# Linear attention and a cosine FFN on one core: another order table for the same steps

## The chip, the cores and the metric

The kernel runs on one core of one Trainium2 chip. The metric is the device time of one execution in microseconds (us); of several executions the median is taken. Engines: PE (TensorE, matmuls), PEld (its weight loads), DVE (VectorE), ACT (ScalarE), POOL (GpSimd) and SP (SyncE, which here issues nearly all DMAs).

## What is computed

Batch 8, 8 heads, 576 tokens a head, head width 64, feature width 128; then a feed-forward part of width 512 to 2048 to 512 over 4608 tokens.

```python
def phi(x):
    proj = np.einsum('bhsd,df->bhsf', x, w_phi)
    proj = proj - np.max(np.abs(proj), axis=-1, keepdims=True)
    return np.concatenate([np.exp(proj), np.exp(-proj)], axis=-1)
q_p, k_p = (phi(q), phi(k))
kv = np.einsum('bhsf,bhsd->bhfd', k_p, v)
z = np.sum(k_p, axis=2)
num = np.einsum('bhsf,bhfd->bhsd', q_p, kv)
den = np.einsum('bhsf,bhf->bhs', q_p, z)[..., None] + 1e-06
x = (num / den)                    # heads side by side: 4608 x 512
h = x @ w_in
g = h * np.cos(h)
out = g @ w_out
```

## The kernel before

The program is first written down as a list of 4103 steps, and nothing is issued while it is written. A step has an engine, a function that issues its instructions, the steps that it needs, and the buffers that it takes or uses: `Step("PE", 0.86, q_mm, [ld], ...)`. Steps are numbered as they are made.

- **Attention**, `attention(u)` for 32 units u of two heads each: steps 0 to 1264, 42 to 39 a unit; the units' qk loads are 0, 42, 83, 124, 165, 206 and so on to 1187 and 1226. A unit loads q and k (`load`, lines 535 to 542, tile `qk`) and v (`load_v`, tile `vs`), projects q (`q_mm`, `q_end`, lines 556 to 562) and k (`k_mm`, `k_end`, lines 597 to 631), takes maxima on DVE, spreads them on POOL, subtracts on POOL (L598), takes exponentials on ACT (`exp_k`, L660 and L663; `exp_q`, L669), and multiplies: `kv_mm` (L709, L715; 32 or 72 narrow matmuls) builds kv and z, `x_mm` (L744, L750; two halves of 32 and 40 narrow matmuls) the output, which DVE divides, transposes and SP stores to `xs` in DRAM.
- **Weights**, `convert(kind, i)`: steps 1265 to 1552. They turn the 64-bit weights into high and low parts of fp32r and store them in DRAM.
- **FFN over three columns of 512 tokens**, `visit(v)`: steps 1553 to 2275. `mm1` (L871, 12 matmuls of 512 columns), then on ACT and DVE `copy`, `reduce`, `cosine`, `times`, `high` and `low`, then `mm2` (L916, L917, 4 matmuls of 512 columns; `one` has 2) and `mm2l` (L923, 2). Partial sums are kept in DRAM (`sums`); `fetch` (L954) loads them, `out_copy` (L959) adds a bank to them and so empties the bank, `out_store` stores them.
- **FFN over six columns in pairs**, `visit_two`: steps 2276 to 4102. With sums of blocks of the operands seven products do the work of eight: `wide` (L1110, 6 matmuls of 512 columns), `turns`, `reduce`, `cosine` and `times`, then `sweep` with `fold_load` (L1267, weights to `wo_h` and `wo_l`), `high`, `low`, `mm2` (L1313, 4) and `mm2l` (L1319, 2).

What sets the order of the work is the list ORDER (lines 88 to 246): a permutation of the 4103 numbers, written out. Steps are issued in that order, so each engine runs its own steps in the order in which ORDER names them, and waits by semaphore for what other engines have to give it. SP's list is a queue in the same way: a DMA whose buffer isn't free holds up those behind it. Buffers turn in rings of one to four (`qk` and `qk_x` one each, `vs` 2, `wo_h` 2, `wo_l` 2, `x_raw` 4, `o` 2), so a load can start when the last reader of the older content is done. `plan()` (line 249) also gives out the eight PSUM banks, along ORDER:

```python
for x in (steps[i] for i in ORDER):
    for b in x.take:
        if b.ring == "bank":
            fit = [i for i in range(len(banks)) if not b.onto or owner[i] and owner[i].kind != "a"]
            b.slot = min(fit, key=lambda i: last(owner[i]))
```

A step gets the bank whose last user stands earliest in ORDER, and waits for that user. ACT holds one table at a time, exp or sin; the loop that issues the steps loads the other one where ORDER asks for it (L1462):

```python
for x in plan():
    if x.eng == "ACT" and x.table not in (None, held_set):
        held_set = x.table
        ACT.preload_act_table(AF.Exp if held_set == "e" else AF.Sin)
    x.fn()
```

PE runs its narrow matmuls on parts of its array; a step of another shape than the one before is a switch of shape.

Steps that the prediction follows: 165, 485 and 1187 are qk loads, and 182, 488 and 1204 are `k_end`, `q_end` and `k_end` of the same units; 289 loads v for the `kv_mm` 317; 2019 is a `fetch` for the `out_copy` 2020 (DVE), 712 an `x_mm` half; 2301 loads a tile of x, 2259 is a `low` (DVE) and 2262 its `mm2l`; 2187 is a `times` (DVE) and 774 a `k_mm`; 3880 and 3881 are `fold_load`s, 3905 the `mm2` that reads 3880. 206, 992 and 2796 are a qk load, another one and a `fold_load`.

Of the kernel before, what the change touches and what calls it, by code (L numbers as in the profile page):

```python
# [26 lines left out]
def phi_attention_then_cos_ffn(ctx: ExitStack, tc: tile.TileContext, qkT, vS, w_phi, w_in, w_out, out, outT):  # L27
# [42 lines left out]
    class Step:  # L70
        def __init__(self, eng, cost, fn, deps=(), take=(), use=(), lat=None, table=None, port=False, kind="", pipe=0.0):
# [10 lines left out]
            for b in self.take + self.use:  # L82
# [6 lines left out]
    ORDER = [0, 3, 5, 4, 7, 8, 6, 9, 10, 11, 42, 58, 60, 62, 44, 1, 12, 46, 2, 17, 19, 18, 23, 24, 1265, 16, 47, 61, 66, 63, 21, 45, 59, 48, 20, 1266, 14, 50, 25,  # L89
# [159 lines left out]
    def plan():  # L249
        place = {steps[x]: i for i, x in enumerate(ORDER)}  # L250
        owner = [None] * len(banks)
# [4 lines left out]

        for x in (steps[i] for i in ORDER):
            for b in x.take:
# [5 lines left out]
                elif b.ring == "v":  # L264
                    b.slot, n_v = n_v, 1 - n_v
        return [steps[i] for i in ORDER]

# [1261 lines left out]
```

## Time and profile before

| | us |
|---|---|
| median of 3 executions (1001.46 to 1005.89) | 1001.76 |
| the profiled execution | 1000.83 |
| its span, first to last instruction | 999.1 |

The profile is of one execution. A page gives busy times by engine, the chain of work that ended last, groups of instructions by line with their mean length and the idle time before them, and DMA issues with the time to landing; the trace behind it gives the timeline of each engine, merged where instructions of one line follow each other, and busy times by stretch. Starts of PE's instructions are recorded, their ends are modelled. TensorE's granted clock was 1.00 throughout.

### The profile page before, as it was taken

The numbers are of one execution on the slowest core, as the hardware profiler recorded it, in microseconds if no ns is written. First come the engines' busy times: TensorE is split into PE (matmuls) and PEld (weight loads), VectorE is DVE, ScalarE is ACT, GpSimd is POOL, SyncE is SP. The second block draws the span as 40 slices with busy tenths as digits, with TensorE's granted clock in tenths as the row PEclk, the third lists the DMA queues.
The fourth block names the chain that finished last, engine by engine and source line by source line (L and its number), as shares of the span: only waits on it lengthen the run. The fifth ranks groups of instructions, "written<-read, shape, count | busy, mean of one in ns | idle before, by whom it ended". The sixth has DMA issues, their size and how long they took to land.

```text
span 999.1 us, 22265 instructions
## 1 busy us (share of the span) xinstructions
PE 985.1 (99%) x8586; PEld 795.6 (80%) x8586; DVE 855.3 (86%) x1494; ACT 769.0 (77%) x1544; POOL 203.3 (20%) x295
## 2 busy tenths in 40 slices
PE   9999999999999999999999999999999999999998
PEld 6778878878888887877788877778878888888786
DVE  7999999999899798777997689987987799776787
ACT  7799999867778866869998779787677775766653
POOL 4564441224332133201223111110200100000000
PEclk9999999999999999999999999999999999999999
DMA  6576788736868675646776546757657485763565
GB/s 234 163 227 179 220 272 287 272 135 226 263 216 274 213 257 188 205 140 247 242 248 198 189 145 197 255 162 256 191 187 231 144 270 182 245 240 102 194 191 187
DMA packets 118745, 211.66 MB, mean 212 GB/s; under 512 B 18672, under 2 KB 61808, under 8 KB 118640
## 3 DMA queue, kind: packets, MB, share of 16 engines
q1 hardware_dynamic: 118496, 210.18, 64.1%
q8 instruction: 67, 1.10, 0.5%
q14 instruction: 38, 0.31, 0.1%
q10 hardware_dynamic: 144, 0.07, 0.0%
HBM read 149.39 MB, written 60.82 MB: 210 GB/s over the span
## 4 chain that ended last, share of the span: by engine, by line
PE 58%; DVE 19%; ACT 11%; DMA 7%; issue 3%; SPq 1%; POOL 1%; DVEq 0%; ACTq 0%; POOLq 0%
PE bank L1110 21%; PE bank L1313 12%; PE bank L1319 6%; PE bank L871 5%; PE bank L744 3%; DVE gl L55 3%; PE bank L709 3%; ACT ek L663 3%; PE bank L605 2%; PE bank L559 2%; DVE bq L594 2%; ACT eq L669 2%; DMA o<-sums 1%; DMA sums<-o 1%; DVE g L895 1%
## 5 line engine op out<-in xcount | busy, mean ns | idle before, releaser
L663 ACT ACTIVATE ek<-bank,mk 128x128 f32<-128x128 f32 x464 | 127.9, 413 | 10.3 <-DVE mk L646 9.9
L598 POOL TENSOR_TENSOR pq<-pq,bq 128x288 f32<-128x288 f32 x128 | 118.5, 954 | 77.9 <-DVE bq L594 59.5
L590 POOL COPY m<-m 32x36 f32<-32x36 f32 x96 | 34.5, 359 | 361.5 <-DVE m L585 357.7
L1313 PE MATMUL bank<-gh,wo_l 128*128 128x512 f32 x336 | 89.3, 394 | 0.4 <-ACT gh L50 0.4
L1313 PE MATMUL bank<-gh,wo_h 128*128 128x512 f32 x336 | 87.4, 394 | 1.3 <-DMA wo_h<-wo_sums 1.3
L669 ACT ACTIVATE eq<-pq 128x576 f32<-128x576 f32 x128 | 80.4, 704 | 3.1 <-POOL pq L598 2.3
L1222 ACT ACTIVATE g<-g,halfpi 128x512 f32<-128x512 f32 x96 | 67.4, 718 | 19.6 <-DVE g L1219 19.3
L1110 PE MATMUL bank<-xh_t,wi 128*128 128x512 f32 x192 | 76.6, 399 | 0.9 <-DVE o L1385 0.3
L744 PEld LDWEIGHTS bank<-kv,eq 128*64 128x64 f32 x2048 | 64.1, 138 | 14.5 <-issue 6.9
L1313 PEld LDWEIGHTS bank<-gh,wo_h 128*128 128x128 f32 x336 | 62.1, 188 | 16.0 <-ACT gh L50 1.9
L1313 PEld LDWEIGHTS bank<-gh,wo_l 128*128 128x128 f32 x336 | 61.9, 188 | 15.4 <-ACT gh L50 2.1
L744 PE MATMUL bank<-kv,eq 128*64 128x65 f32 x2048 | 70.0, 223 | 1.1 <-DVE o L959 1.1
L709 PEld LDWEIGHTS bank<-vs,ek 128*64 128x64 f32 x2048 | 62.7, 138 | 8.3 <-ACT ek L663 1.9
L709 PE MATMUL bank<-vs,ek 128*64 128x65 f32 x2048 | 66.8, 223 | 0.9 <-ACT pq L570 0.9
L1219 DVE SCALAR_TENSOR_TENSOR g<-g,hs 128x512 f32<-128x512 int32 x72 | 51.6, 722 | 13.8 <-ACT g L1216 13.3
L1462 ACT ACT_TABLE_LOAD x48 | 61.6, 1283 | 0.8
L1120 ACT ACTIVATE hs<-bank 128x512 f32<-128x512 f32 x72 | 42.2, 597 | 23.2 <-PE bank L1110 19.1
L1216 ACT ACTIVATE g<-hs 128x512 int32<-128x512 f32 x72 | 45.7, 637 | 17.7 <-DVE hs L1134 11.3
L916 PE MATMUL bank<-wo_h,gh 128*128 128x512 f32 x144 | 57.4, 399 | 0.0
L1110 PE MATMUL bank<-xh_b,wi 128*128 128x512 f32 x144 | 56.9, 395 | 0.0
L1110 PE MATMUL bank<-x_wi,wi 128*128 128x512 f32 x144 | 56.2, 390 | 0.0
L917 PE MATMUL bank<-wo_l,gh 128*128 128x512 f32 x144 | 56.2, 390 | 0.0
(186 smaller groups left out, 2626.0 us busy)
## 6 DMA issues: line engine op xcount, KB each, us to landing
wi<-wi_parts SPq DMA_DIRECT2D x18, 1792.0 KB, 8.1
qk<-qkT SPq DMA_DIRECT2D x31, 640.0 KB, 4.9
wo_h<-wo_sums SPq DMA_DIRECT2D x24, 512.0 KB, 4.5
wo_l<-wo_sums SPq DMA_DIRECT2D x24, 512.0 KB, 4.3
x_raw<-xs SPq DMA_DIRECT2D x47, 256.0 KB, 4.1
wi_parts<-wi SPq DMA_DIRECT2D x12, 896.0 KB, 6.1
vs<-vS SPq DMA_DIRECT2D x32, 325.0 KB, 5.5
wo_l<-wo_parts SPq DMA_DIRECT2D x18, 512.0 KB, 6.0
```

What stands on the lines that cost most here:

```text
L598: qeng.tensor_tensor(out=d["pq"][:, c], in0=d["pq"][:, c], in1=d["bq"][:, c], op=ALU.subtract)
L663: ACT.activation(out=e[:, g, s * P:(s + 1) * P], in_=pk[:, g, :], func=AF.Exp, scale=1.0 - 2.0 * s, bias=d["lk" if s == 0 else "mk", i][:, ...
L669: ACT.activation(out=e[:, s, :], in_=d["pq"][:, j * S:(j + 1) * S], func=AF.Exp, scale=1.0 - 2.0 * s)
L709: PE.matmul(out=acc[c:c + 64, n, i, :], lhsT=e[:, s, P * n + c:P * n + c + 64], rhs=vs[b["v"].slot][:, 2 * s + i, :], start=(s == 0 and i ...
L744: PE.matmul(out=ps[64 * h:64 * h + 64, 65 * g:65 * g + 65], lhsT=d["eq", j][:, n, c:c + 64], rhs=d["kv"][:, 2 * n + j, :], start=h not in ...
L916: PE.matmul(out=bank(acc[tb]), lhsT=n["gh"][:, t], rhs=w[:, 0, r], start=first, stop=False, skip_group_check=True)
L917: PE.matmul(out=bank(acc[tb]), lhsT=n["gh"][:, t], rhs=w[:, 1, r], start=False, stop=False, skip_group_check=True)
L1110: PE.matmul(out=bank(bank_b), lhsT=w[:, part, block, j * P:(j + 1) * P], rhs=d[x, name, j], start=start and k == 0, stop=k == 5, skip_grou ...
L1222: ACT.activation(out=n["g"], in_=n["g"], func=AF.Sin, bias=halfpi, scale=1.0)
L1313: PE.matmul(out=bank(out[j]), lhsT=w[:, place, part, j * P:(j + 1) * P], rhs=n["gh"], start=start and i == mine[0] and part == 0, stop=Fal ...
L1319: PE.matmul(out=bank(out[j]), lhsT=w[:, place, 0, j * P:(j + 1) * P], rhs=n["gl"], start=False, stop=i == mine[-1], skip_group_check=True)
L1462: ACT.preload_act_table(AF.Exp if held_set == "e" else AF.Sin)
```

## The change

One thing changes: the list ORDER. It holds the same 4103 numbers in another sequence, the outcome of a new search over four sets of step lengths in which the lengths of steps of all engines scatter. The steps, their functions, the ring sizes and `plan()` stay. 259 of PE's 1017 steps keep their place in PE's own list; the others move by a few places, 25 at most. On ACT the largest move is 42 places, on DVE 58, on POOL 7 and on SP 64. Since banks and table loads follow from ORDER, some steps get another bank, and the table is loaded at other places. The diff, cut to lines of the list that the prediction speaks of (all other lines of the list change too):

```diff
--- before.py
+++ after.py
@@ -86,164 +86,164 @@
 
     SWITCH = dict(e=1.3, s=1.3, full=0.23, left=0.147, quarter=0.138, upper=0.195)
     SHAPE = dict(mm1="full", mm2="full", mm2l="full", one="full", onel="full", wide="full", k_mm="upper", k_end="full", q_end="full", k_sub="full", kv_mm="left", x_mm="left", q_mm="upper")
-    ORDER = [0, 3, 5, 4, 7, 8, 6, 9, 10, 11, 42, 58, 60, 62, 44, 1, 12, 46, 2, 17, 19, 18, 23, 24, 1265, 16, 47, 61, 66, 63, 21, 45, 59, 48, 20, 1266, 14, 50, 25,
...
-             54, 87, 89, 88, 91, 55, 1272, 34, 35, 90, 104, 69, 72, 57, 73, 165, 182, 108, 101, 74, 106, 109, 1273, 56, 92, 36, 1274, 37, 93, 70, 102, 187, 107,
...
-             314, 203, 368, 261, 289, 293, 296, 262, 308, 240, 332, 239, 260, 312, 241, 259, 309, 277, 242, 278, 345, 275, 274, 331, 279, 297, 1555, 313, 204,
-             1304, 1563, 333, 349, 1305, 347, 348, 281, 317, 1558, 350, 318, 205, 1561, 335, 334, 243, 353, 1564, 354, 298, 299, 302, 280, 330, 303, 316, 1562,
...
-             452, 1629, 422, 453, 436, 462, 1614, 420, 402, 1627, 1628, 1630, 466, 1334, 463, 468, 467, 485, 1612, 1631, 464, 403, 1299, 287, 469, 419, 454, 421,
-             465, 435, 434, 455, 456, 488, 437, 1338, 1339, 1340, 1341, 1336, 447, 471, 1281, 1632, 1644, 472, 470, 1645, 457, 487, 1633, 489, 439, 490, 1646, 404,
...
-             1511, 2145, 672, 2027, 709, 2019, 735, 674, 1512, 2070, 2071, 675, 707, 2020, 676, 1460, 739, 740, 760, 737, 710, 762, 2028, 712, 2029, 677, 711, 713,
...
-             2185, 2186, 2187, 1533, 774, 2134, 2137, 778, 779, 749, 799, 801, 802, 751, 759, 2217, 2152, 776, 750, 752, 753, 754, 1551, 2277, 2135, 2153, 2139,
...
-             2294, 2229, 2230, 2194, 2257, 2303, 2258, 839, 2301, 842, 2240, 2241, 2306, 2312, 2251, 2313, 2307, 2320, 2321, 2267, 2323, 2195, 2308, 2309, 2250,
-             2260, 2310, 2259, 2314, 2311, 2322, 2315, 2317, 2318, 2196, 2252, 2262, 2316, 2264, 843, 841, 844, 845, 2319, 2324, 2327, 2325, 2329, 2328, 2268,
...
-             1152, 2845, 1154, 1138, 2850, 2848, 2852, 1153, 2911, 2839, 1156, 2906, 1139, 1187, 1155, 2909, 1157, 2916, 2854, 2858, 1204, 2851, 1168, 2859, 1158,
...
-             3884, 3878, 3885, 3886, 3888, 3889, 3890, 3891, 3879, 3791, 3898, 3907, 3899, 3792, 3793, 3881, 3893, 3894, 3895, 3900, 3896, 3901, 3902, 3903, 3904,
-             3880, 3905, 3912, 3906, 3877, 3908, 3910, 3913, 3915, 3510, 3928, 3909, 3697, 3914, 3876, 3911, 3917, 4003, 3916, 3932, 3924, 3918, 3920, 3919, 3921,
...
-             4080, 4085, 4050, 4051, 4090, 4092, 4093, 4094, 4095, 4096, 4097, 4098, 4099, 4100, 4101, 4102]
+    ORDER = [0, 3, 5, 4, 7, 8, 42, 58, 6, 9, 10, 44, 1, 62, 45, 60, 17, 46, 1265, 11, 12, 18, 21, 59, 15, 13, 43, 47, 48, 61, 22, 66, 19, 20, 71, 1266, 64, 2, 23,
...
+             86, 72, 1282, 73, 105, 87, 55, 165, 89, 88, 1272, 90, 106, 74, 57, 35, 91, 34, 84, 1273, 70, 54, 92, 1274, 109, 127, 36, 102, 93, 1275, 1276, 141, 69,
...
+             96, 98, 144, 133, 111, 1279, 182, 185, 206, 134, 40, 135, 110, 77, 223, 184, 186, 1283, 187, 78, 189, 188, 125, 79, 228, 145, 168, 80, 167, 191, 1284,
...
+             1302, 259, 289, 308, 260, 307, 1558, 297, 275, 1563, 1303, 277, 1297, 240, 278, 309, 312, 239, 274, 1555, 203, 330, 1304, 345, 241, 349, 347, 279,
+             331, 281, 1305, 1564, 313, 333, 242, 350, 348, 317, 318, 1561, 1306, 319, 280, 123, 334, 1562, 298, 354, 299, 302, 353, 1307, 332, 303, 243, 346, 205,
...
+             1609, 1610, 417, 418, 463, 449, 1329, 1330, 433, 1613, 468, 1621, 448, 1622, 469, 1611, 1331, 365, 450, 1625, 462, 1623, 1332, 452, 464, 485, 451,
+             420, 1624, 453, 1612, 465, 1334, 400, 1629, 1626, 1630, 1627, 1628, 472, 466, 399, 401, 454, 436, 402, 422, 467, 419, 434, 1615, 366, 421, 1631, 488,
...
+             729, 561, 674, 675, 707, 709, 2024, 735, 1510, 1517, 2019, 2026, 760, 2048, 710, 1511, 2073, 712, 2062, 1512, 676, 677, 711, 2049, 737, 730, 738,
+             1514, 762, 2208, 739, 740, 763, 2020, 2078, 1518, 1519, 713, 2079, 714, 743, 2089, 2100, 744, 1424, 761, 764, 2206, 1520, 2050, 715, 2051, 2052, 2053,
...
+             2187, 2276, 2215, 2135, 2188, 749, 2211, 774, 2216, 2217, 2138, 778, 779, 750, 801, 1543, 1544, 1545, 1546, 2176, 2277, 776, 777, 773, 2189, 2139,
...
+             2297, 827, 2200, 841, 2303, 2255, 2256, 2312, 2196, 2313, 2320, 2301, 2307, 2201, 2257, 1551, 2258, 2322, 2251, 2252, 2267, 839, 2202, 2308, 1497,
+             2309, 2310, 2311, 2321, 2317, 842, 2441, 2326, 2259, 2323, 2314, 2315, 2316, 2324, 2327, 2341, 2342, 2264, 2325, 2260, 2329, 2318, 2319, 2343, 2328,
+             2330, 852, 2345, 2337, 2331, 837, 2344, 2338, 2339, 2332, 854, 875, 2262, 2349, 2346, 2333, 2268, 2334, 2350, 855, 2351, 2347, 2352, 2261, 843, 856,
...
+             1170, 2910, 2838, 2906, 2911, 2909, 2839, 1171, 2854, 2847, 2848, 2852, 2849, 2912, 1168, 2856, 1140, 1187, 1174, 1107, 1172, 2907, 1141, 2855, 1069,
+             1169, 2851, 2913, 2858, 1159, 2860, 1173, 2919, 1204, 2853, 2920, 2859, 2917, 1142, 1162, 1143, 1209, 1210, 1190, 1144, 1163, 2857, 1161, 2861, 2864,
...
+             3888, 3912, 3885, 3897, 3973, 3875, 3890, 3889, 3898, 3880, 3893, 3895, 3900, 3894, 3902, 3881, 3903, 3886, 3907, 3908, 3899, 3891, 3896, 3901, 3792,
+             3993, 3913, 3793, 3917, 3876, 3904, 3757, 3877, 3905, 3910, 3511, 3915, 3918, 3988, 3906, 3909, 3920, 3940, 3914, 3911, 3916, 3919, 3928, 3929, 3924,
...
+             4092, 4094, 4090, 4093, 4095, 4097, 4096, 4098, 4099, 4100, 4101, 4102]
     LATENCY = dict(PE=0.35, ACT=0.25, DVE=0.2, POOL=0.25, SP=2.0)
 
     def plan():
```

## Rows read from the trace of the kernel before

**Rows 1.** The page: the span and the busy time of each engine.
```profile
span 999.1 us, 22265 instructions
...
PE 985.1 (99%) x8586; PEld 795.6 (80%) x8586; DVE 855.3 (86%) x1494; ACT 769.0 (77%) x1544; POOL 203.3 (20%) x295
```

**Rows 2.** The chain that ended last (start us, us, what): a stretch of products.
```profile
664.02 14.98 PE bank L1110 x66
```

**Rows 3.** Timeline of PE at ten places: start us, us, instruction, [idle before <-releaser].
```profile
24.98 0.46 PE L630 MATMUL bank<-wphi,qk 128*128 128x128 f32 x2 [0.30 <-DMA qk<-qkT]
...
74.55 2.09 PE L709 MATMUL bank<-vs,ek 128*64 128x65 f32 x64 [0.92 <-ACT pq L570]
...
126.59 0.46 PE L562 MATMUL bank<-qk,wphi 128*128 128x128 f32 x2 [0.39 <-DVE m L584]
...
163.20 0.96 PE L871 MATMUL bank<-xh_b,wi 128*128 128x512 f32 x3
...
339.77 1.15 PE L744 MATMUL bank<-kv,eq 128*64 128x65 f32 x32 [1.06 <-DVE o L959]
...
391.65 1.04 PE L605 MATMUL bank<-wphi,qk 64*128 64x128 f32 x13 [0.67 <-DVE g L902]
...
441.36 0.61 PE L923 MATMUL bank<-wo_h,gl 128*128 128x512 f32 x2
442.99 0.73 PE L923 MATMUL bank<-wo_h,gl 128*128 128x512 f32 x2 [1.02 <-DVE gl L55]
...
652.99 0.46 PE L630 MATMUL bank<-wphi,qk 128*128 128x128 f32 x2 [1.08 <-DMA qk<-qkT]
...
836.89 0.50 PE L1110 MATMUL bank<-xh_t,wi 128*128 128x512 f32 x1 [0.32 <-DVE o L1385]
...
942.67 1.07 PE L1319 MATMUL bank<-gl,wo_l 128*128 128x512 f32 x4
945.03 1.15 PE L1313 MATMUL bank<-gh,wo_h 128*128 128x512 f32 x4 [1.29 <-DMA wo_h<-wo_sums]
```

**Rows 4.** The chain that ended last: five loads in it.
```profile
19.91 4.93 DMA qk<-qkT
...
335.39 3.52 DMA o<-sums
...
436.32 3.91 DMA x_raw<-xs
...
647.03 5.82 DMA qk<-qkT
...
938.78 6.12 DMA wo_h<-wo_sums
```

**Rows 5.** Timeline of PE: two halves of x_mm, then a product.
```profile
513.27 1.15 PE L744 MATMUL bank<-kv,eq 128*64 128x65 f32 x32
...
514.48 1.10 PE L744 MATMUL bank<-kv,eq 128*64 128x65 f32 x32
515.52 1.67 PE L1313 MATMUL bank<-gh,wo_l 128*128 128x512 f32 x6
```

**Rows 6.** The page's DMA issues: count, KB each, median us to landing.
```profile
qk<-qkT SPq DMA_DIRECT2D x31, 640.0 KB, 4.9
wo_h<-wo_sums SPq DMA_DIRECT2D x24, 512.0 KB, 4.5
```

**Rows 7.** The page's groups: table loads (busy us, mean ns, idle before).
```profile
L1462 ACT ACT_TABLE_LOAD x48 | 61.6, 1283 | 0.8
```

**Rows 8.** Timeline of ACT: one table load and what follows.
```profile
413.71 1.28 ACT L1462 ACT_TABLE_LOAD   x1
415.00 1.26 ACT L669 ACTIVATE eq<-pq 128x576 f32<-128x576 f32 x2
```

**Rows 9.** Busy us of each engine by stretch (length, then each engine, clock, DMA).
```profile
0.00:185.00 185.00, 182.04 (x2611) 143.76 (x2612) 169.71 (x330) 168.52 (x377) 80.79 (x126) 1.00 0.69 222
185.00:475.00 290.00, 286.69 (x2271) 233.71 (x2271) 252.30 (x404) 219.81 (x413) 73.36 (x99) 1.00 0.66 222
```

284 rows, old and new, of the table ORDER are left out of this document.

## The prediction

> **What bounds the kernel now.** I read the page's busy times first: PE is busy for 985.1 of 999.1 us, DVE for 855.3, ACT for 769.0 [rows 1]. That looks like a kernel with 14 us to win at most, but the end of a matmul is modelled, so a wait can hide inside "busy". The second view therefore goes by starts: in the chain of waits 66 matmuls of 512 columns take 14.98 us [rows 2], 0.227 us each. Wherever two starts of PE lie further apart than the steps between them need, PE stood still. Laid against this spacing, and against the usual length of each narrow step, PE is late by more than 0.16 us at 20 places, 12.7 us together. One is the first load of the program (0.33 us), which no order removes; 12.4 us are left. The rest of the span is the same matmuls in any order, plus hiccups of about 0.13 us at some hundred places that no step of the table explains. So the change can win 12.4 us at the most, and it can lose as much as it likes.
>
> **Where the 12.4 us lie.** Eight places hold 8.1 us [rows 3]. At 942.67 us four matmuls need 0.91, so the next was due at 943.58; it started at 945.03, 1.45 late. At 441.36 two need 0.45, the next came at 442.99 instead of 441.81, 1.18 late. By the same account 24.98 is 0.37 late, 74.55 is 1.14, 126.59 is 0.66, 339.77 is 1.13, 391.65 is 0.94 and 652.99 is 1.24. Eleven smaller ones of 0.17 to 0.55, from 163.20 to 836.89, make 4.3. What ended the big ones stands in the chain of waits [rows 4]: five times a load landed just before (4.93 us after its issue at 19.91, 3.52 at 335.39, 3.91 at 436.32, 5.82 at 647.03, 6.12 at 938.78); at 339.77 and 442.99 DVE, which the view of rows 3 names, only passed the late load on. The starts 74.55 and 126.59 are named after ACT and DVE, but come 0.14 us after a qk or vs load landed, as 24.98, 652.99 and 945.03 do. Only 391.65 waits for DVE alone.
>
> **The change part by part.** No instruction is added or removed but six table loads; all else is a new order on each engine. I read from the two tables what PE work stands between a load and its first PE reader, and call that its lead.
>
> *Six of the eight places.* Step 1187 (qk load) and its reader 1204 had no PE step between them; now an x_mm half (1.0 us [rows 5]) and an mm2 step (four matmuls, 0.91) stand there: 1.9 us against 1.24 late. 165 and 182 stood side by side; now 15 PE steps are between, six of them of some 1.0 us, against 0.37 late. 3880 and 3905: from nothing to two mm2 and four mm2l, 3.6 us, against 1.45; 3880 also goes ahead of 3881 now instead of behind it. 485 and 488: from one mm1 (2.7) to one mm1, two x_mm halves and a kv_mm, at least 6.0, against 0.66. 2259 and 2262: from one mm2l to over 6 us, against 1.18. Step 712 waited because it took the bank that 2020 empties; 2020 now comes after 712, so plan() gives 712 another bank: 1.13. Sum 6.0 us, if nothing else becomes late.
>
> *Two places stay.* 289 keeps its lead to 317 (7.0 to 6.7 us), and 2187 still stands ahead of 774 with no PE step between: 2.1 us remain. The eleven small waits for DVE and ACT (4.3 us) I leave as they are: the table doesn't thin the chains behind them in one direction.
>
> *What comes instead.* A load with a lead of up to 0.5 us is thin. Without the first three units, the old table has 17 of them and the new 21. Three of the 17 waited for longer than 0.16 us, 3.06 us together, 0.18 per thin load; at that rate the 21 cost 3.8. The other end is zero, and it has a reason: a load that runs ahead of its place in the table is safe if its buffer was freed early. For 165 and 1187 the matmuls between the freeing step and the reader are only 4.8 us against landings of 4.93 and 5.82 [rows 4]. Of the new 21 the shortest, 2796, has 5.2 us, where such a load takes 4.5 in the median and a qk load 4.9 [rows 6]. I take the middle, 1.9, because that margin is small beside landings of up to 6.12 us. The three other removed waits (0.66, 1.18 and 1.13, together 3.0) came from crowding on the SP queue and on DVE, which a new order creates elsewhere: between 0 and 3.0, I take 1.5.
>
> *Switches.* PE changes its tile shape 156 times instead of 154. An x_mm half ahead of another one takes 0.98 us, ahead of a full-size matmul 1.04 [rows 5]; so at about 0.1 each 0.2 us. ACT switches its table 54 times instead of 48, each 1283 ns [rows 7]; from its start to the next one (413.71 to 415.00) are 1.29 us [rows 8], so six are 7.7 us of ACT time. Counted by PE work, all six fall between 175 and 450 us, that is in the stretch 185 to 475, where ACT is busy for 219.8 of 290 us; none falls in the first 185 us, where it is busy for 168.5 and DVE for 169.7 [rows 9]. 70 us of idle ACT cover 7.7, so I cost them at nothing; without that cover they are 7.7 on the path.
>
> The page "ScalarE: Activation LUTs" of the Trainium skill, section "What ACT_TABLE_LOAD costs", speaks against the change: it adds a drain of about 1380 ns to the same 1283, 2.66 us a switch, and advises batching by table set. By it the six would be an estimated 16 us of ACT. No such drain shows here: the next instruction starts 0.01 us behind the load.
>
> *Sum.* -6.0 + 1.9 + 1.5 + 0.2 = -2.4 us. The profiled execution took 1000.83 (span 999.1 and 1.8 around it), which becomes 998.4; the median of the runs lies 0.93 above the profiled one, so I say 999.4.
>
> **The rivals.** A measurement of this kernel can tell about 0.5% from no change: faster is below 996.75, slower above 1006.77.
>
> *Most waits go.* If none of the thin loads waits and the crowding doesn't come back, and the small waits shrink too, two thirds of 12.4 go: 1001.76 - 8.3 = 993.5; all of them would give 989.4. For it: six of the eight large places are cured with leads well above their lateness, and no freed buffer is shorter than its usual landing any more. Against it: two large places are not cured, and there are more thin leads.
>
> *The waits only change places.* 12.4 us go and 12.4 come: 1001.76 + 0.2 = 1002.0. For it: 17 thin loads against 21. Against it: two of the old 17 had a buffer freed too late, none of the new has.
>
> *The table loads land on the path.* Place: ACT between 185 and 475 us. A sin chain (turns, reduce, cosine, times, high) or an exp that feeds PE has to wait for 1.29 us per load, and PE with it where it has no other product ready. All six on the path: 999.4 + 7.7 = 1007.1, slower than before; with the waits only changing places four of the six would do for 1006.8. For it: ACT there is idle mostly in waits for DVE, and a load that comes just ahead of a due cosine is not moved into them. Against it: 24% of ACT's time is idle there, and PE's big waits in this stretch were for loads and DVE.
>
> With the page's 2.66 us a load, three on the path would decide for slower, and six would give about 1015; as the trace shows no drain, I give that no chance of its own.
>
> **How the numbers follow.** The forecast 0.36, waits change places 0.16 (both within 0.5%, together 0.52), most waits go 0.34 (faster), table loads on the path 0.14 (slower). The likeliest gives 999.4; its own range is 996.8 to 1002. Over the cases the range goes from 990.5 (nearly all waits gone) to 1006.5: some 0.05 lie below it, some 0.1 above.
>
> **What would show it.** Right: no idle of PE over 0.5 us ahead of the readers of 165, 485, 1187, 3880, nor at 712 and 2262; a wait of about 1 us still at 317 and 774; 54 table loads in all but no PE wait on ACT over 1 us between 185 and 475 us; late starts of 9 to 11 us in all, some at loads with thin leads, such as 2796, 206 and 992. Wrong: starts late by under 6 us in all (then the cure is wider than I say) or over 16 (then crowding or the table loads decide), or a PE whose spacing within a step is no longer 0.227 us.

## The result, and the profile after

The new table takes 992.96 us in the median of 4 runs (991.68 to 994.18), the old one on the same chip 1003.58 (1001.46 to 1005.89): ratio 0.9894, 95% interval 0.9862 to 0.9925. It is faster by about 1%. The profiled execution of the new table took 994.18 us, span 992.5, where the one of before took 1000.83 and 999.1: 6.6 us of the 10.6 show between the two profiles. Two single executions of the old table took 1833.88 and 2506.94 us; the ratios and counts below leave them out.

The page of after: the span, the busy times (answer to [rows 1]), the chain that ended last by engine, and the table loads (answer to [rows 7]).

```profile
span 992.5 us, 22281 instructions
...
PE 982.0 (99%) x8586; PEld 796.5 (80%) x8586; DVE 852.5 (86%) x1494; ACT 777.9 (78%) x1550; POOL 200.8 (20%) x295
...
PE 92%; DVE 4%; DMA 2%; ACT 1%; issue 1%; SPq 0%; DVEq 0%; ACTq 0%
...
L1462 ACT ACT_TABLE_LOAD x54 | 69.3, 1283 | 0.9
```

The same line of the page of before, the chain that ended last by engine:

```profile
PE 58%; DVE 19%; ACT 11%; DMA 7%; issue 3%; SPq 1%; POOL 1%; DVEq 0%; ACTq 0%; POOLq 0%
```

The work is the same and six table loads more; what changed is the chain: 92% of it is PE now, where it was 58%.

The timeline of PE in after, at the places where before had its big waits ([rows 3]); a wait would stand in brackets at the end of a line.

```profile
25.08 0.49 PE L562 MATMUL bank<-qk,wphi 128*128 128x128 f32 x2
...
35.80 0.61 PE L630 MATMUL bank<-wphi,qk 128*128 128x128 f32 x4
...
74.35 0.86 PE L709 MATMUL bank<-vs,ek 128*64 128x65 f32 x22 [0.52 <-ACT ek L663]
...
126.54 0.38 PE L562 MATMUL bank<-qk,wphi 128*128 128x128 f32 x2
...
338.19 1.15 PE L744 MATMUL bank<-kv,eq 128*64 128x65 f32 x32
...
390.91 1.06 PE L605 MATMUL bank<-wphi,qk 64*128 64x128 f32 x16
...
447.05 0.62 PE L923 MATMUL bank<-wo_h,gl 128*128 128x512 f32 x2
...
651.68 0.38 PE L630 MATMUL bank<-wphi,qk 128*128 128x128 f32 x2
...
938.74 2.00 PE L1313 MATMUL bank<-gh,wo_h 128*128 128x512 f32 x8
```

Steps 182 (at 35.80), 488, 712, 774, 2262, 1204 and 3905 start when PE's step before them is done. Only the `kv_mm` 317 at 74.35 still waits, and no longer for its load but for an exponential. New waits stand elsewhere; these are the two largest, with the chain's load behind the first:

```profile
626.04 0.70 PE L1313 MATMUL bank<-gh,wo_h 128*128 128x512 f32 x2 [1.64 <-DMA wo_h<-wo_sums]
...
734.09 0.73 PE L1313 MATMUL bank<-gh,wo_l 128*128 128x512 f32 x2 [1.20 <-ACT gh L50]
```

```profile
618.04 0.92 PE bank L1319 x4
618.96 0.02 issue
618.98 6.92 DMA wo_h<-wo_sums
625.90 0.14 issue
626.04 2.08 PE bank L1313 x8
```

The load is 2796, which the prediction named as the one with the shortest cover: its buffer came free at 618.96, it was issued at once, and it took 6.92 us to land.

By the prediction's account (from one PE start to the next, less what the steps between usually take; the usual lengths are now medians over all profiles), before was late by more than 0.16 us at 20 places, 12.9 us together, and after at 11 places, 7.8 us. With the smaller ones the sums are 38.1 and 31.4 us; the difference, 6.7, is about that of the spans, 6.6.

### The profile page after: what moved, and what is told of

Read it like the earlier page. It is cut to its first block, busy times and chain, and to the rows that moved or that the text cites. A ratio compares the mean times of both kernels' runs of the same rounds, so it can differ in the third digit from the quotient of the medians.

```text
span 992.5 us, 22281 instructions
## 1 busy us (share of the span) xinstructions
PE 982.0 (99%) x8586; PEld 796.5 (80%) x8586; DVE 852.5 (86%) x1494; ACT 777.9 (78%) x1550; POOL 200.8 (20%) x295
## 4 chain that ended last, share of the span: by engine, by line
PE 92%; DVE 4%; DMA 2%; ACT 1%; issue 1%; SPq 0%; DVEq 0%; ACTq 0%
PE bank L1110 23%; PE bank L1313 14%; PE bank L871 12%; PE bank L1319 7%; PE bank L744 6%; PE bank L709 5%; PE bank L916 4%; PE bank L923 4%; PE bank L917 4%; PE bank L605 3%; PE bank L559 3%; PE bank L715 1%; PE bank L651 1%; DVE gl L55 1%; PE bank L630 1%
## 5 line engine op out<-in xcount | busy, mean ns | idle before, releaser
L598 POOL TENSOR_TENSOR pq<-pq,bq 128x288 f32<-128x288 f32 x128 | 115.6, 932 | 121.6 <-DVE bq L594 103.2
L643 DVE TENSOR_REDUCE mk<-bank 128x4 f32<-128x512 f32 (+1 forms) x96 | 51.0, 541 | 6.5 <-PE bank L630 3.3
L1110 PE MATMUL bank<-x_raw,wi 128*128 128x512 f32 x144 | 56.1, 390 | 0.0
```

The lines of the kernel that those rows point to most:

```text
L598: qeng.tensor_tensor(out=d["pq"][:, c], in0=d["pq"][:, c], in1=d["bq"][:, c], op=ALU.subtract)
L1110: PE.matmul(out=bank(bank_b), lhsT=w[:, part, block, j * P:(j + 1) * P], rhs=d[x, name, j], start=start and k == 0, stop=k == 5, skip_grou ...
```

## The experiments

Each ratio is to the kernel before, run beside it on the same chip. In the diffs a line is a piece of ORDER with the steps of one engine alone. A move that a step's inputs force on other engines is in them too. The first theory was the prediction's: the gain is that of the cured waits, one by one.

**Seven waits cured in the old table.**

```diff
 PE
-73, 182, 102, 127, 140, 126, 181
+73, 102, 127, 140, 126, 182, 181
-2839, 1204, 2849, 2856, 2860, 2853
+2839, 2849, 2856, 2860, 1204, 2853
 SP
-1622, 1621, 1614, 1334, 485
+1622, 485, 1621, 1614, 1334
-122, 1298, 329, 163, 1556, 368, 289
+122, 1298, 289, 329, 163, 1556, 368
-3881, 3880
+3880, 3881
 DVE
-187, 38
+38, 187
-2308, 2309, 2259
+2259, 2308, 2309
-675, 2020, 676, 739, 740, 737
+675, 676, 739, 740, 737, 2020
```

> The old table with seven local moves and nothing else: k_end 182 four places later and k_end 1204 three places later on PE, 485 three and 289 four places earlier on SP, 3880 ahead of 3881 on SP, low 2259 two places earlier on DVE, and out_copy 2020 placed behind 712 so that 712 gets another bank. Theory A (a wait for a late load is local; what is won there is kept): the late starts at these seven places, 7.2 us in all, go and nothing comes back: about 7 us below the kernel before, ratio 0.992 to 0.994. Rival B (the waits move: what PE wins at one place it stands still for later): under half is kept, ratio 0.996 or above, with new late starts within some 50 us behind each cured place.

Measured: 1000.56 us (before 1003.27), ratio 0.9971, interval 0.9956 to 0.9987. All seven waits (7.2 us) are gone from its trace, and only 2.7 us from the time. Up to 460 us its PE was late by 23.8 us in all (before 20.7), after that by 15.0 (before 17.4). So the cures of the second half were kept, and those of the first were not. Of the late starts up to 460 us, 1.7 us stand behind a fall of TensorE's clock in this one execution (more on that below).

**Whose order is it: SP's, or the others'?** Two tables were merged from the two: SP's steps in their new order and all others in the old (first run), and the reverse (second). The merges aren't pure: the two orders don't fit everywhere, and steps were moved until they did. In the first, 55 of SP's 462 steps lie off their new places (by 8 at most), and 33 of PE's, 26 of ACT's and 104 of DVE's off their old ones (by 8, 6 and 23 at most); in the second it is 38 of SP's (6), 16 of PE's (5), 44 of ACT's (6) and 82 of DVE's (21).

```diff
-ORDER: SP old; PE, ACT, DVE, POOL old
+ORDER: SP new; PE, ACT, DVE, POOL old; moved where they don't fit
```

> SP's queue in the order of the changed table, the other engines in the order of the old one (moves of one or two places where a buffer demands it). Theory A1 (it took moves on several engines; at 182 and 1204 PE's order decides, at 712 and 2262 DVE's place): only 488 and 3905 are cured, new mismatches between loads and readers come: no faster than the kernel before, ratio 0.997 to 1.005. Rival C (the gain is the order of the DMA queue): most of the gain is here, ratio 0.989 to 0.993.

Measured: 1065.34 us, ratio 1.0613, interval 1.0587 to 1.0638.

```diff
-ORDER: SP old; PE, ACT, DVE, POOL old
+ORDER: SP old; PE, ACT, DVE, POOL new; moved where they don't fit
```

> PE, ACT, DVE and POOL in the order of the changed table, SP's queue in the order of the old one. Theory A1: the cures by PE's and DVE's order are here (182, 1204, 712, 774, 2262: about 5 us), some of it lost to loads that now stand too late in the queue: ratio 0.993 to 1.000. Rival C (the DMA queue's order decides): no gain, ratio 1.000 or above.

Measured: 1082.52 us, ratio 1.0802, interval 1.0768 to 1.0837. Either merge costs 6 to 8%, which neither expectation had foreseen: here a queue's order was good only with the engines that it was laid out with. How much of this is due to the moves that made the two orders fit isn't shown. From the chain of the first of the two:

```profile
270.40 6.55 DMA sums<-o
276.95 0.02 issue
276.97 5.45 DMA o<-sums
282.41 0.03 issue
```

A store holds its buffer for 6.55 us, the `fetch` that takes it can't start before, and the `out_copy` behind it frees PE's bank only at the end. Such long waits of PE cost more than their own length. The windows of the first kernel, then of the second, each with a wait in it (length, then PE, PEld, DVE, ACT, POOL busy, PE's granted clock, DMA share, GB/s):

```profile
275.00:281.00 6.00, 2.52 (x69) 2.25 (x64) 0.00 (x0) 2.91 (x7) 0.00 (x0) 1.00 0.45 129
281.00:287.00 6.00, 3.75 (x9) 2.98 (x10) 4.39 (x5) 0.00 (x0) 0.00 (x0) 0.50 0.02 8
```

```profile
500.00:505.00 5.00, 1.75 (x8) 1.10 (x6) 2.26 (x3) 3.60 (x11) 3.05 (x4) 1.00 0.63 212
505.00:511.00 6.00, 2.75 (x40) 2.55 (x42) 1.94 (x5) 0.89 (x3) 0.00 (x0) 0.50 0.57 187
```

In both kernels PE has stood idle for some 3 us when the granted clock falls to 0.50, that is 1.2 instead of 2.4 GHz, and what comes next runs at half speed. That an idle PE is set to half its clock is also what the Trainium skill says, page "TensorE: Matmul & The Clock Gate", section "Part 1: The HAM clock gate (the "warmup" mystery)"; the rows agree.

**Which half of the table gains?** The new order for the first 2000 places and the rest in the old order, and the reverse.

```diff
-ORDER = old
+ORDER = new[:2000] + [i for i in old if i not in new[:2000]]
```

> The first 2000 places of the changed table, then the remaining steps in the order of the old table (the cut lies at some 440 us of PE work, 460 us of time). Theory E (many thin arrivals: in the profile of the kernel before 112 steps of PE got their last input less than 0.4 us ahead of their start, in that of the changed kernel 68; each waits now and then, and what is won is spread along the table): each half brings a part, here 3 to 7 us below the kernel before, ratio 0.993 to 0.997, and this one and its counterpart add up to about the whole change. Rival B (what one stretch wins the next one gives back, since the old table stands still where the engines behind PE catch up): nothing is left at the end, ratio 0.998 or above.

Measured: 996.51 us (before 1004.88), ratio 0.9922, interval 0.9899 to 0.9945: some 8 us, more than was expected.

```diff
-ORDER = old
+ORDER = old[:2000] + [i for i in new if i not in old[:2000]]
```

> The counterpart: the first 2000 places of the old table, then the remaining steps in the order of the changed one. Theory E: 3 to 7 us below the kernel before, ratio 0.993 to 0.997, and with the other half about 10 us. Rival F (the gain lies in the first half, where ACT and DVE are busy for over nine tenths): no faster than before, ratio 0.999 or above, and the other half has it all.

Measured: 1001.75 us, ratio 0.9971, interval 0.9950 to 0.9992. The halves add up: 0.78% and 0.29% make 1.07%, and the whole table gave 1.06%. Some three quarters of the gain come from the first 2000 places, in which five single cures gained nothing (below).

**Are table loads free?** Three kernels were to issue table loads twice: the new table's 29 between 183 and 475 us, its 11 up to 175 us, and the old table's 23 between 183 and 480 us. The diff is that of the first; the others have 66 and 1724, and 1724 and 900, as bounds.

```diff
+        first, last = ORDER.index(1724), ORDER.index(899)
+        again = {steps[i] for i in ORDER[first:last]}
...
-                ACT.preload_act_table(AF.Exp if held_set == "e" else AF.Sin)
+                for _ in range(2 if x in again else 1):
+                    ACT.preload_act_table(AF.Exp if held_set == "e" else AF.Sin)
```

> The changed kernel, with each of its 29 table loads between 183 and 475 us issued twice: 29 more loads of 1283 ns, 37 us more of ACT, in a stretch in which ACT has some 60 to 70 us idle. Theory A (ACT's idle time covers table loads, so the six that the change added cost little): PE waits for ACT at a few places, 0 to 10 us above the changed kernel, 0.0 to 0.35 us a load, and so at most 2 us for the six. Rival D (a table load lands on the path, because it stands just ahead of an exp or a sin that is due): 1.28 us a load, some 37 us above the changed kernel.

> The new table with its 11 table loads between 10 and 175 us issued twice: 14.1 us more ACT in a stretch of 185 us in which ACT has 14.3 us idle. Theory (in this stretch ACT has no room, and what comes late there reaches PE): 4 to 12 us more than the new table, ratio to the kernel before 0.993 to 1.001. Rival (table loads are free on this kernel wherever they stand, as 29 of them between 183 and 475 us were): ratio 0.989.

> The kernel before, with each of its 23 table loads between 183 and 480 us issued twice: 23 more loads of 1283 ns, 30 us more of ACT. Theory E (the old table's arrivals are thinner, so the same disturbance of ACT that cost the changed kernel nothing reaches PE here): 3 to 12 us above the kernel before, ratio 1.003 to 1.012. Rival A (ACT's idle time covers them, whatever the order): ratio 0.998 to 1.002.

Measured: 992.21 us (ratio 0.9892, 0.9870 to 0.9913), 992.22 (0.9876, 0.9851 to 0.9901) and 1003.42 (0.9993, 0.9974 to 1.0013). But the second load never ran. The groups of the three pages, in that order:

```profile
L1465 ACT ACT_TABLE_LOAD x54 | 69.3, 1283 | 0.9
```

```profile
L1465 ACT ACT_TABLE_LOAD x54 | 69.3, 1283 | 0.9
```

```profile
L1465 ACT ACT_TABLE_LOAD x48 | 61.6, 1283 | 0.8
```

54, 54 and 48 loads, as without the edit: a load of the table that is already held leaves no instruction. So these runs say nothing of the price of a table load; none of the three expectations was tried, and the second is wrong to take the first run for a sign that loads are free. They are three more measurements of the two unchanged kernels: over 14 runs in all the new table takes 992.2 us in the median (990.9 to 994.2). Their traces also tell which waits recur. In all three executions of the new table step 3163 waits (1.38, 1.38, 1.38 us), as do 1574 (0.85, 0.81, 0.82), 317 (0.74, 0.73, 0.75), 22, 2228 and 3441. 2800, which reads the load 2796, waits 1.81, 0 and 0.90: a load's time is what varies.

**Seven waits cured in the new table.** If the new table's gain were a matter of single waits, its own could be cured in the same way.

```diff
 DVE
-3157, 3160
+3160, 3157
-1320, 1584, 1604
+1584, 1604, 1320
-12, 21
+21, 12
-1303, 309, 203, 1304, 241, 349, 347, 1305, 1564
+309, 203, 241, 349, 347, 1564, 1303, 1304, 1305
 ACT
-1302, 275, 1563, 312, 274, 279, 313
+275, 1563, 312, 274, 279, 313, 1302
 SP
-2766, 2796
+2796, 2766
-3412, 3437, 3436
+3436, 3412, 3437
-2298, 2299, 2194
+2194, 2298, 2299
```

> The changed table with seven more local moves at its own late starts: g_sum 3160 ahead of low 3157 (DVE, for 3163), w.bits 1320 behind times 1604 (DVE, for 1574), w.scale 1302 behind exp_k 313 (ACT, for 317), k_max 21 ahead of q_turn 12 (DVE, for 22), and on SP the loads 2796, 3436 and 2194 ahead of two loads or fetches each. Their late starts are 6.1 us in the profile of the changed kernel; five of them, 4.0 us, came back within 0.3 us in a second profile with the same order. Theory E (a cure is kept where arrivals behind it aren't thin): some half is kept, 2 to 3 us below the changed kernel, 0.987 of the kernel before. Rival B (waits move): none is kept, equal to the changed kernel within 1 us.

Measured: 995.83 us (993.76 to 1005.55), ratio 0.9919, interval 0.9891 to 0.9946: no gain on the new table (992.2 over its 14 runs), and rather some 3 us lost. The weight step 1302, moved on ACT behind an exponential, took the DVE steps 1303 to 1305 with it, which need it. They now stand together shortly ahead of the small DVE step 350 (`k_neg`) and start only at 75.32, when 1302 is done. So 350 ends at 78.41 here and at 75.26 in the new table; the exponential 354 needs it, and PE waited for that at 80.73. The timeline of PE and the windows behind it:

```profile
78.71 0.39 PE L630 MATMUL bank<-wphi,qk 128*128 128x128 f32 x2
80.73 1.48 PE L871 MATMUL bank<-xh_b,wi 128*128 128x512 f32 x3 [1.63 <-ACT ek L663]
```

```profile
80.00:81.00 1.00, 0.27 (x1) 0.27 (x2) 1.00 (x2) 1.00 (x5) 0.00 (x0) 0.98 0.47 37
81.00:82.00 1.00, 1.00 (x3) 0.70 (x3) 1.00 (x2) 1.00 (x5) 0.36 (x1) 0.50 0.55 188
```

Again the clock falls behind the wait, for 3.4 us, and three matmuls take 1.48 us where three at full clock take 0.85 (a row below). Of the 10 runs eight have a mean granted clock of 0.998 or less. Another cure only handed its wait on: with 3160 ahead of 3157, step 3163 no longer waits, but 3159, which needs 3157, starts 1.2 us late:

```profile
737.03 0.72 PE L1319 MATMUL bank<-gl,wo_h 128*128 128x512 f32 x2 [0.93 <-DVE gl L55]
```

**Early cures and late cures apart.** The cures of the first experiment, split at 460 us.

```diff
 PE
-2839, 1204, 2849, 2856, 2860, 2853
+2839, 2849, 2856, 2860, 1204, 2853
 SP
-3881, 3880
+3880, 3881
```

> The old table with two of its waits of PE mended, both from the second half: PE c.k_end 1204 three places later (it waited 1.64 us at 694 us for its DVE step) and the x_raw load 3880 ahead of 3881 (its PE step 3905 waited 1.4 us at 967 us). Theory (where PE alone is the bound, a wait that is mended stays mended): 2.0 to 3.0 us less, ratio 0.997 to 0.998. Rival (a mended wait comes back somewhere later, wherever it lay): ratio 0.9995 to 1.0005.

Measured: 1000.43 us (before 1003.32), ratio 0.9962, interval 0.9944 to 0.9980. (The expectation gives two waits wrongly; they are the 1.24 us at 652.99 and the 1.45 at 945.03 of [rows 3], 2.7 together.) The medians differ by 2.9.

```diff
 PE
-73, 182, 102, 127, 140, 126, 181
+73, 102, 127, 140, 126, 182, 181
 SP
-1622, 1621, 1614, 1334, 485
+1622, 485, 1621, 1614, 1334
-122, 1298, 329, 163, 1556, 368, 289
+122, 1298, 289, 329, 163, 1556, 368
 DVE
-187, 38
+38, 187
-2308, 2309, 2259
+2259, 2308, 2309
-675, 2020, 676, 739, 740, 737
+675, 676, 739, 740, 737, 2020
```

> The old table with five of its waits of PE mended, all before 460 us (PE b.k_end 182 four places later, SP loads 485 and 289 earlier, DVE m.low 2259 earlier, DVE m.out_copy 2020 behind 712): 4.5 us of waits by its own trace. Theory (where ACT and DVE are over 90% busy the waits come back elsewhere, since a wait of PE is what lets them catch up): ratio 0.998 to 1.002, and its trace shows new late starts before 185 us that make up for at least half. Rival (a mended wait stays mended): ratio 0.9955.

Measured: 1002.88 us, ratio 0.9990, interval 0.9974 to 1.0005: at most 2.6 us of the 4.5 were kept, and as likely none. About half of them came back soon after. In this trace, and in that of the seven cures, three steps start late that are on time in before, in its repeat and in the kernel with late cures alone: 225 by 0.8 us in both, 1565 by 0.55 here and 1.0 there, and 2324 by 1.0 here and 0.4 there. That is 2.3 us of the 4.5 in either. The three in this kernel:

```profile
50.31 1.12 PE L651 MATMUL bank<-mk,minus 128*128 128x512 f32 x2 [0.98 <-DVE mk L643]
...
79.99 0.96 PE L871 MATMUL bank<-xh_b,wi 128*128 128x512 f32 x3 [0.30 <-ACT ek L663]
...
446.59 0.50 PE L1110 MATMUL bank<-xh_t,wi 128*128 128x512 f32 x1 [0.94 <-ACT bank L1128]
```

In before, the last input of each had come only 0.06 to 0.08 us ahead of its start, so a PE that isn't held up before them waits there; 2324 stands right behind the cured 2262.

The rest is scatter as much as loss. Before 185 us this kernel's PE was late by 13.2 us (before 10.5), so 2.7 us more although 2.2 had been cured there; but the kernel with late cures alone, whose order up to there is the old one, also shows 13.9. The wait that grew is the same in both, ahead of step 1697 ([rows 3], 163.20: 0.55 us). Its timeline in the kernel with late cures, then in the one with early cures:

```profile
163.93 1.16 PE L605 MATMUL bank<-wphi,qk 64*128 64x128 f32 x14 [1.59 <-ACT o L963]
165.02 1.65 PE L871 MATMUL bank<-xh_b,wi 128*128 128x512 f32 x3
```

```profile
165.16 1.16 PE L605 MATMUL bank<-wphi,qk 64*128 64x128 f32 x14 [1.96 <-ACT o L963]
166.25 0.96 PE L871 MATMUL bank<-xh_b,wi 128*128 128x512 f32 x3
167.05 0.39 PE L871 MATMUL bank<-xh_t,wi 128*128 128x512 f32 x1
167.28 0.85 PE L871 MATMUL bank<-xh_b,wi 128*128 128x512 f32 x3
```

And the window of the first and of the second behind the wait:

```profile
166.00:167.00 1.00, 1.00 (x4) 0.77 (x3) 1.00 (x2) 0.82 (x4) 0.00 (x0) 0.50 1.00 394
```

```profile
166.00:167.00 1.00, 1.00 (x7) 0.79 (x6) 0.61 (x2) 1.00 (x2) 0.00 (x0) 1.00 0.92 373
```

The order up to there is the same in before, in its repeat and in the kernel with late cures, and yet 1697 is late by 0.5, 1.3 and 2.1 us; in the last of them the clock then fell for 3.4 us, which made the next step late by another 1.7. In the kernel with early cures, after a longer wait, it didn't. The old table meets such a drop often. Of 66 of its runs beside the experiments, 22 had a mean granted clock of 0.998 or less (a drop of 3.4 us takes 0.0017 off the mean), with a median of 1006.4 us; the 44 others have 1003.2. Of the new table's 14 runs none had less than 0.999. Six traces have the old order up to 185 us, but for single cures, and three of them show a drop there; of the five with the unchanged new order there none does.

**The new table with two late cures.**

```diff
 DVE
-3141, 1198, 3155, 3152, 3157, 3160
+3141, 3155, 3152, 3157, 3160, 1198
 SP
-3412, 3437, 3436
+3436, 3412, 3437
```

> The new table with two late waits of its second half mended: DVE q_turn 1198 behind g_sum 3160 (PE's step 3163 waited 1.38 us at 734 us) and the load fold_load 3436 two places earlier on SP (3441 waited 0.42 us at 818 us). Theory (a mended wait in the second half is kept): 1.2 to 1.8 us less than the new table, ratio to the kernel before 0.987 to 0.988. Rival (waits move on): the new table's own ratio, 0.989.

Measured: 990.73 us (989.84 to 991.86), ratio 0.9865, interval 0.9841 to 0.9890, where the unchanged new table took 992.22 (990.86 to 993.10) beside it. Both waits are gone from its trace (three of 0.24 to 0.28 us came), and 1.5 us from the median; the intervals overlap, so its lead over the new table is likely rather than certain. It is the quickest kernel of this study. What the first move did is seen on DVE. From the timeline of the new table, then of this kernel:

```profile
729.56 2.52 DVE L55 TENSOR_TENSOR gl<-g_wi_x,gh 128x512 fp32r<-128x512 f32 x2
730.28 3.67 POOL L598 TENSOR_TENSOR pq<-pq,bq 128x288 f32<-128x288 f32 x3
732.01 1.29 DVE L1277 TENSOR_TENSOR g_wi_x<-g_wo_xl,g_wi_x 128x512 f32<-128x512 f32 x1
```

```profile
729.77 3.84 POOL L598 TENSOR_TENSOR pq<-pq,bq 128x288 f32<-128x288 f32 x4 [43.31 <-DVE bq L594]
...
730.12 1.30 DVE L55 TENSOR_TENSOR gl<-g_wi_x,gh 128x512 fp32r<-128x512 f32 x1
...
732.02 0.68 DVE L1229 TENSOR_TENSOR g_pq_x<-bank,g 128x512 f32<-128x512 f32 x1
...
735.39 0.69 DVE L55 TENSOR_TENSOR gl<-g_qk,gh 128x512 fp32r<-128x512 f32 x1 [0.30 <-ACT gh L50]
```

The DVE step L55 takes 0.69 us by itself and 1.26 to 1.30 beside POOL's subtractions, for which `q_turn` 1198 gives the start. In the new table three such steps in a row stood in front of 3163, some 0.6 us longer each; with `q_turn` behind them they are done before POOL begins.

## Why the prediction held, and which steps failed

The range held the time; the likeliest case, 999.4 and no change that can be measured, was not what came. The case "most waits go" came nearest, with 993.5 for a measured 992.96, but that its number fits is partly luck: it took 8.3 us off 1001.76, and between the profiles the large late starts fell by 5.1 us, while the old table's median came out at 1003.58. Of that case's three conditions only one came true, that the small waits shrink; a thin load did wait, and crowding came back. The range held also because it is wide, 16 us; the likeliest case lies 6.4 us above the measured time.

Its steps, by the profiled executions, late starts over 0.16 us alone (us):

| step | forecast | found |
|---|---|---|
| six places cured | -6.0 | -6.0 |
| two places stay (317, 774) | 0 | -1.4 |
| eleven small waits stay | 0 | -4.4 |
| loads with thin leads | +1.9 | +1.8 (0 and 0.9 in the two repeats) |
| crowding elsewhere | +1.5 | +4.2 (eight places; 3163 alone 1.4) |
| first loads of the program | 0 | +0.7 |
| sum | -2.6 | -5.1 |

- **The six cures** came as worked out: a lead well above the lateness was enough at each.
- **"The eleven small waits for DVE and ACT (4.3 us) I leave as they are: the table doesn't thin the chains behind them in one direction"** is the step that failed most. None of the eleven is in the new trace. PE takes about 1000 steps whose last input comes from another engine; that input was less than 0.4 us old at 112 of them in before and at 68 in after. The leads of loads alone, which the prediction compared (17 against 21), didn't show that; one count over all inputs, DVE's and ACT's too, needs both traces.
- **Two places stay.** 774 doesn't: the `q_mm` 799 now stands ahead of it, and its `times` 2187 ended at 389.10, 1.81 us before 774 started; in before it ended at 391.60, after the step's first start at 390.50. The prediction looked for PE steps between 2187 and 774 alone, and not for what else had moved ahead of 774. 317 keeps 0.74 of 1.14, for another reason.
- **Loads with thin leads.** The 1.8 for a forecast 1.9 is all at 2800: load 2796 had a cover of 5.2 us and took 6.92. The repeats have 0 and 0.9, so the match is luck. That a cover is longer than the usual landing, as the prediction found for all new loads, doesn't keep out a slow one.
- **Crowding** was sized too low, and its largest piece is none of the kinds named: DVE beside POOL.
- **Table loads.** 54, as said, and between 185 and 475 us no PE wait is longer than 0.39. With the six more, ACT is busy for 233.1 of 290 us there, 13.3 more than in before ([rows 9]), of which the six loads are 7.7:

```profile
185.00:475.00 290.00, 289.79 (x2354) 237.81 (x2353) 251.67 (x410) 233.10 (x428) 72.92 (x98) 1.00 0.71 238
```

The rival "table loads land on the path" falls by the time. What one costs by itself wasn't measured.
- **From the profile to the median.** That "the median of the runs lies 0.93 above the profiled one" rested on three runs. Over the 66 runs the old table's median is 1003.6, as in the four beside the new table, 2.8 above its profiled execution; the new table's profiled one is 1.2 above the median of its four runs. These 4.0 and the 6.6 between the profiles are the 10.6 measured. A part of the 2.8 is the clock: the runs without a drop have 1003.2. The other 2.4 lie in executions without a profile, and what is late in them stays open.
- **Late starts of 9 to 11 us** were expected; 7.8, and 5.3 and 5.9 in the repeats: the repeats are under the 6 us that the prediction had set as the sign that "the cure is wider than I say".

That single cures are kept where PE alone is the bound is shown for two in the old table (2.9 us of 2.7) and is likely for two in the new; the move of 3160, in the same stretch, was not kept, so it also takes a move that delays nothing PE is about to need. That the new table gains in the first half because it has fewer thin arrivals fits the counts (110 after the seven cures, 93 and 86 with one half new) and the three waits that came back behind cured ones, but it was not shown for the table as a whole: the new table with seven cures also has 68, and is slower.

## What to carry to other kernels

Judge a new order by all arrivals at the bound engine and not by the waits that one trace happens to show: one and the same wait was 0.5 us in one execution and 2.1 in another. Move the queue of loads and the engines together: tables with one in the old order and the other in the new cost 6 to 8% here. Before mending a single wait, look at the inputs of the steps behind it: if they come only just in time, the wait moves there, as it did for half of 4.5 us here. Try such mends first where one engine alone is busy, and look for the added instruction in the trace before reading the time of an experiment.

## What the runs showed of the hardware that was not expected

- An idle time of PE of 1.5 to 1.6 us (at 163.93 and 80.73 above, and in the seven cures at 164.91) was followed by 3.4 us at half clock, which cost 1.7 us more at 163.93 and 164.91; one of 1.96 us at 165.16 was not.
- DVE and POOL: a DVE step that reads two tiles of SBUF took 1.26 to 1.30 us beside POOL's subtraction and 0.69 without; one that reads a bank took 0.68 beside it as well. The Trainium skill, page "SBUF — State Buffer", section "SBUF: two separate sides", says that DVE with two SBUF inputs and a GpSimd operation that reads SBUF share a pair of ports, and that the one that comes second is blocked. The trace agrees; what the DVE step lost was some 0.6 us each time. POOL lost too: a subtraction took 1.1 to 1.26 us beside such steps and 0.81 beside DVE steps that read a bank.
- A load of the table that ACT already holds leaves no instruction in the trace: 54, 54 and 48 of 83, 65 and 71 asked for. Whether the chip or the building of the program drops it isn't shown.
